# Gated attention plus expert block: the order in which three weight combinations are loaded before the last stage, and two more small products at the start

## The chip, the cores and the metric

The kernel runs on one core of a Trainium2 chip. The metric is device microseconds of one execution, launch to end; lower is better. Before the change three executions took 1855.58, 1856.39 and 1862.57 us (median 1856.39). A fourth, run under the profiler, took 1856.62 us, of which its span (first to last instruction of the program) is 1854.8 us; the other 1.8 us lie around it.

## The reference, cut to what matters

```python
def reference(A_x, A_wqkv, A_wo, B_x, B_w_q, B_k1, B_k2, B_u, B_v, gate_w):
    x = A_x                                        # 1 x 2048 x 1024, f32
    g = _sigmoid((x * gate_w).sum(-1, keepdims=True))
    a = _A_ref(x, A_wqkv, A_wo)                    # 32 heads of 32: softmax(q k^T) v, then @ wo
    b = _B_ref(x, B_w_q, B_k1, B_k2, B_u, B_v)     # 64 experts, one chosen per head, gelu
    return g * a + (1 - g) * b
```

The last operation of `a` is a product of a 2048 x 1024 matrix `o` (the heads' outputs, normalised and gated) with the 1024 x 1024 weight `wo`. `b` ends in a product of a small matrix of expert weights with `v`, added into the same sums.

## The kernel before, in words

All matrix products are done in split precision: an operand is cut into a high part (ScalarE, `split`, L93) and the rest, a low part (VectorE, L94), and a product is high x high + high x low + low x high. So one 128-row product over a depth of 512 is 12 TensorE instructions of 128x512.

**Start.** `wqkv` and `x` arrive in pieces (`load_w0`, `load_x`), are split, and the first projection runs in the loop `mm0` (L213): for each of eight 128-deep slices of `x`, 24 products. The slice `kc=0` goes column block by column block, the others go part by part. While the first pieces travel, TensorE multiplies the identity by itself nine times (L208 and L209; each f32 product of this kind stands as two instructions in the trace). The results are overwritten.

**Middle.** The remaining projections, the expert router, the values, and attention over 32 heads.

**Last stage (from L1154).** The 2048 rows of `o` are done in eight chunks of 256 rows, n = 0 to 7. Chunks 0 and 1 are multiplied plainly by `wo` (`wo_mm`, L1173, into the PSUM banks `pa` and `pa1`; `av_mm`, L1180, adds the expert part). Chunks 2 to 7 go through `unit(n)`: each is a 2x2 block product done with seven block products in place of eight (class `Halves`; `product`, L617). The seven are issued in the order P1, P7, P5, P6, P2, P3, P4 (P3, P4, P2 at the end of the last chunk). Their left factors are blocks of the chunk and sums of blocks, computed and split per chunk (`operand`: A11, S3, S1, A12, S2, S4, A22). Their right factors are blocks of `wo`, which are in SBUF, and four combinations T1 to T4 of blocks of `wo`, made during the values stage, split, and kept in DRAM as `t0h`, `t0l` (T1), `t1h`, `t1l` (T2), `t2h`, `t2l` (T3), `t3h`, `t3l` (T4), high and low part of each. `FACTORS` (L573) pairs them: P7 is S3 with T3, P5 is S1 with T1, P6 is S2 with T2, P4 is A22 with T4.

Each part of a combination is 1 MB (128 rows of 8 KB). `load_t(i, ...)` loads T(i+1) into places that have become free: T1 into the tiles `wo_raw0`, `wo_raw1`, T2 into `wo_raw2`, `wo_raw3` (which held the unsplit `wo`), the high part of T3 into `z0`, its low part into a tile of its own, `t3l`, and T4 into halves of `woh` and `wol`, 512 columns at a time. In the trace the DRAM tensor `t3l` and the tile `t3l` have one name: `t3l<-t2l` loads T3's low part, `wol<-t3l` a piece of T4's.

`load_o(n)` loads chunk n of `o` (tile `V`, eight transfers of 128 KB), `load_rb(n)` its row factors (tile `accd`, four transfers of 256 KB, or small ones for a single slice), `load_at(n)` the expert weights (`at`). `scale_o(n)` multiplies `o` by the factors (L1225). `plain_out(n, pa)` copies the four banks of a plain chunk into the tile `post` (trace: `rb`; L1233 on ScalarE, L1235 on VectorE) and stores it, four stores `out<-rb` of 256 KB. Both plain chunks use the same `post`, so the copies of chunk 1 wait until the stores of chunk 0 have landed. They are called in `unit(2)` after P1 and stand, in the order of both engines, ahead of the operands S2, S4 and A22 of chunk 2.

**Queues.** The order of instructions on each engine is the order of the program, written out by hand. Nearly all loads and stores are issued by SyncE (SP) in one queue; `load_rb(3)` is issued by ScalarE. Every transfer of these two queues takes the next of eight completion counters in turn, and its issue waits until the counter's last user has landed. A waiting issue holds up everything behind it on its queue. Before the change the queue of SP around the change reads: t0h, t0l, t1h, t1l, the eight pieces of chunk 2's `o`, `at`, t2h, t2l, the four stores of chunk 0, the eight pieces of T4, the eight pieces of chunk 3's `o`. The four transfers of `load_rb(3)` take their counters in between: the fourth piece of chunk 2's `o` waits for the first of them, the fifth for the second, the seventh for the third.

The names that the prediction uses: L208/L209 and L213 at the start; `load_t` (L1212), the calls at L1273, L1284 to L1292, `plain_out` (L1230), `unit` (L1310).

Of the kernel before, what the change touches and what calls it, by code (L numbers as in the profile page):

```python
# [10 lines left out]
F32R = mybir.dt.float32r  # L11
# [5 lines left out]
S = 2048  # L17
# [14 lines left out]
def gated_mha_peer_kernel(ctx, tc, xT, wqkv, wv, wo, wq, k12, ug, v, out):  # L32
# [26 lines left out]
    TD = [[dram.tile([128, KC // 2, 512], F32R, name=f"t{i}{part}") for part in "hl"] for i in range(4)]  # L59
# [13 lines left out]
    def dma(dst, src, queue=nc.sync):  # L73
        a, b = (ap.bitcast(F32) if ap.dtype == F32R else ap for ap in (dst, src))
        return queue.dma_start(a, b)
# [76 lines left out]
    def pair(pool, name, m):  # L152
        return [pool.tile([128, m * 512], F32R, name=part + name) for part in ("hi", "lo")]
# [51 lines left out]
    b0 = {(w, n): bank() for w in range(2) for n in range(NQ)}  # L205


    for i in range(9):  # L208
        nc.tensor.matmul(b0[1, NQ - 1][:, :128], ident, ident, start=True, stop=True)  # L209

    def mm0(w, n, kc, i):
# [4 lines left out]
    for kc in range(KC):  # L216
# [17 lines left out]
        for w in range(2):  # L234
            for n, i in order:
                mm0(w, n, kc, i)
            if kc == KC - 1:
                parts = pair(ev0, str(w), NQ)
# [316 lines left out]
    zp = Pool("zp", side="right")  # L555
# [344 lines left out]
    keep = Pool("keep")  # L900

    wo_raw = [keep.tile([128, 2, D], F32, name=f"wo_raw{i}") for i in range(KC // 2)]
# [196 lines left out]
    for h in range(H):  # L1099
        base = h * NT  # L1100
        g, j = divmod(h, 4)
# [52 lines left out]
    fin = Pool("fin")  # L1154
# [9 lines left out]
    def load_at(n):  # L1164
        AT[n] = fin.tile([128, W], F32R, name="at", bufs=3)
        dma(AT[n], ATD[:, n * W:(n + 1) * W])
# [43 lines left out]
    ht = Halves(lambda name: wk.tile([128, 512], F32, name="ssb"), bank)  # L1210

    def load_t(i, *parts):  # L1212

        ht.b[f"T{i + 1}"] = []
        for part, src in zip(parts, TD[i]):
            m = HC // len(part)
            for j, place in enumerate(part):
                dma(place, src[:, m * j:m * j + m, :].rearrange("p k m -> p (k m)"))
            ht.b[f"T{i + 1}"].append([place[:, k * 512:(k + 1) * 512] for place in part for k in range(m)])

    def scale_o(n):

# [20 lines left out]
    def banks4():  # L1243
        return {(i, half): bank() for i in range(W // 128) for half in range(2)}
# [25 lines left out]

    for i in range(2):  # L1273
        load_t(i, *([keep.tile([128, S], F32R, name=f"wo_raw{2 * i + j}")] for j in range(2)))
    ps_odd = Pool("ps_odd", space=PSUM)
    for (i, half), ps in pa.items():
        av_mm(0, i, half, ps)
# [5 lines left out]
        split_o(1, k0, k1)  # L1283
    load_o(2, 0, KC)  # L1284
    load_at(2)
    load_t(2, [zp.tile([128, S], F32R, name="z0")], [fin.tile([128, S], F32R, name="t3l")])
    pa1 = banks4()
    wo_mm(pa1, 1, list(range(KC - 1)), True, False)
    for (i, half), ps in pa1.items():
        av_mm(1, i, half, ps)  # L1290
    plain_out(0, pa)
    load_t(3, *([part[k][:, 512:] for k in range(HC)] for part in (woh, wol)))  # L1292
    load_rb(3, 0, KC, queue=nc.scalar)
    load_o(3, 0, KC)
# [123 lines left out]
```

## Time and profile before

| what | value |
|---|---|
| median of three executions | 1856.39 us |
| the profiled execution | 1856.62 us |
| its span | 1854.8 us |
| TensorE busy in the span | 1843.4 us (99%) |
| VectorE, ScalarE busy | 1365.7 us (74%), 1198.9 us (65%) |
| DMA, mean over the span | 179 GB/s |

How to read it: times are us from the first instruction. PE is TensorE's matmuls, PEld its weight loads, DVE VectorE, ACT ScalarE, SPq and ACTq the issuing of transfers by SyncE and ScalarE. A row of a timeline has the start, the time taken, engine, line, operation, output and inputs, shape and count; in brackets the engine's idle time before it and what ended it. Successive matmuls overlap, so the distance between their starts is their cost, not their stated length. In a table by windows the columns are the window, its length, busy time and count of an engine, the clock that TensorE was granted (1.00 is full), the busy share of the DMA engines and their GB/s.

### The profile page before, as it was taken

What the parts mean: (1) busy time and instruction counts of PE and PEld (TensorE: products, weight loads), DVE (VectorE), ACT (ScalarE), POOL (GpSimd) and SP (SyncE); (2) the same over time, 40 slices, a digit from 0 to 9 for tenths busy, and PEclk for the clock granted to TensorE, in tenths of its full rate; (3) what the DMA queues carried; (4) which work ended last, traced back from release to release, by engine and by line L of the source; (5) the groups of instructions that cost most, each with busy time, mean ns of one, the idle gap of its engine ahead of it and who ended that gap; (6) DMA issues with size and microseconds to landing.
All of it is one profiled execution on the core that took longest, in us unless ns stands there. A gap on an engine that the chain in (4) does not pass through costs nothing.

```text
span 1854.8 us, 26123 instructions
## 1 busy us (share of the span) xinstructions
PE 1843.4 (99%) x10127; PEld 1130.9 (61%) x10127; DVE 1365.7 (74%) x1219; ACT 1198.9 (65%) x1492; POOL 170.1 (9%) x214
## 2 busy tenths in 40 slices
PE   9999999999999999999999999999999999999999
PEld 7877777887888744444444444444444444447787
DVE  4522224978887788888888888888888888895674
ACT  4211111201233399999999999999999999993221
POOL 0000000025401100000000000000000000000000
PEclk9999999999999999999999999999999999999999
DMA  5777784423237687767777777777777777766861
GB/s 215 281 251 255 273 290 135 134 66 104 80 127 247 246 182 160 177 153 176 163 175 176 163 183 170 184 160 183 172 172 169 159 176 177 182 147 196 273 171 57
DMA packets 122853, 332.10 MB, mean 179 GB/s; under 512 B 15988, under 2 KB 57220, under 8 KB 98472
## 3 DMA queue, kind: packets, MB, share of 16 engines
q1 hardware_dynamic: 85048, 180.58, 32.2%
q0 software_dynamic: 17584, 112.08, 28.0%
q10 hardware_dynamic: 20096, 37.76, 6.6%
q8 instruction: 80, 1.31, 0.3%
q14 instruction: 45, 0.37, 0.1%
HBM read 158.65 MB, written 72.10 MB: 124 GB/s over the span
## 4 chain that ended last, share of the span: by engine, by line
PE 85%; issue 6%; DMA 4%; DVE 3%; POOL 1%; ACT 1%; SPq 0%; ACTq 0%; DVEq 0%; POOLq 0%
PE ring L968 28%; PE o L989 25%; PE bk L329 17%; PE pa L617 6%; PE bk L394 3%; PE bk L213 2%; PE bk L274 2%; PE ring L1002 1%; DMA accd<-rd 1%; POOL eq L408 1%; PE pa L1180 1%; DMA t3l<-t2l 1%; DMA rb<-rd 1%; DMA t1l<-xl 1%; DMA smd<-ssb 0%
## 5 line engine op out<-in xcount | busy, mean ns | idle before, releaser
L978 ACT ACTIVATE P<-ring 128x1024 f32<-128x1024 f32 (+2 forms) x1031 | 913.0, 982 | 13.5 <-DMA accd<-P 1.2
L1018 DVE TENSOR_TENSOR acc<-acc,P 128x2048 f32<-128x2048 f32 x319 | 731.0, 2292 | 74.6 <-ACT P L978 49.0
L989 PE MATMUL o<-P,V 128*32 128x512 f32 x3840 | 464.8, 599 | 0.0
L968 PE MATMUL ring<-Q,K 98*128 98x512 f32 x1024 | 272.0, 407 | 0.1
L968 PE MATMUL ring<-z,z 98*128 98x512 f32 x1020 | 270.5, 407 | 0.6 <-ACT accd L978 0.6
L968 PEld LDWEIGHTS ring<-Q,K 98*128 98x128 f32 x1024 | 182.0, 188 | 144.2 <-ACT P L978 72.4
L968 PEld LDWEIGHTS ring<-z,z 98*128 98x128 f32 x1020 | 181.4, 188 | 142.5 <-ACT P L978 72.5
L989 PEld LDWEIGHTS o<-P,V 128*32 128x32 f32 x3840 | 98.8, 109 | 223.3 <-issue 214.4
L93 ACT ACTIVATE hi<-bk 128x512 fp32r<-128x512 f32 x64 | 37.6, 598 | 243.2 <-PE bk L329 227.1
L94 DVE TENSOR_TENSOR lo<-bk,hi 128x512 fp32r<-128x512 f32 x64 | 44.1, 690 | 182.7 <-ACT hi L93 178.5
L329 PE MATMUL bk<-xh,whi 128*128 128x512 f32 x448 | 176.2, 393 | 0.1
L329 PE MATMUL bk<-xh,wlo 128*128 128x512 f32 x448 | 174.4, 389 | 0.0
L329 PE MATMUL bk<-xl,whi 128*128 128x512 f32 x448 | 174.4, 389 | 0.0
L1011 POOL DMA_DIRECT2D accd<-P x95 | 81.5, 858 | 929.4 <-ACT P L978 421.4
L1016 DVE TENSOR_TENSOR acc<-P,P 128x2048 f32<-128x2048 f32 x32 | 73.4, 2293 | 72.9 <-ACT P L978 72.9
L329 PEld LDWEIGHTS bk<-xh,whi 128*128 128x128 f32 x448 | 84.1, 188 | 24.2 <-issue 6.7
L329 PEld LDWEIGHTS bk<-xh,wlo 128*128 128x128 f32 x448 | 84.1, 188 | 17.7
L329 PEld LDWEIGHTS bk<-xl,whi 128*128 128x128 f32 x448 | 84.2, 188 | 16.9
L1021 DVE TENSOR_TENSOR acc<-acc,accd 128x2048 f32<-128x2048 f32 x32 | 73.1, 2285 | 0.0
L978 ACT ACTIVATE accd<-ring 128x1024 f32<-128x1024 f32 (+2 forms) x64 | 62.2, 1032 | 2.5 <-PE ring L968 2.4
L617 PE MATMUL pa<-woh,acc 128*128 128x512 f32 x192 | 62.2, 389 | 0.0
L398 ACT ACTIVATE xu<-bk 128x64 f32<-128x64 f32 x16 | 3.6, 224 | 76.5 <-PE bk L394 71.6
(246 smaller groups left out, 1868.0 us busy)
## 6 DMA issues: line engine op xcount, KB each, us to landing
accd<-P POOLq DMA_DIRECT2D x95, 1024.0 KB, 7.5
wqt<-in_wq SPq DMA_DIRECT2D x32, 1024.0 KB
z<-kdh SPq DMA_DIRECT2D x32, 256.0 KB
z<-qdh SPq DMA_DIRECT2D x32, 256.0 KB
V<-vd SPq DMA_DIRECT2D x32, 256.0 KB
K<-kdh SPq DMA_DIRECT2D x32, 256.0 KB
Q<-qdh SPq DMA_DIRECT2D x32, 256.0 KB
od<-osb SPq DMA_DIRECT2D x32, 256.0 KB
```

The costliest lines, as they stand in the source:

```text
L93: nc.scalar.activation(hi, src, AF.Copy)
L94: (on or nc.vector).tensor_tensor(out=lo, in0=src, in1=hi.bitcast(F32), op=OP.subtract)
L329: nc.tensor.matmul(ps, a[:, kc, :], b[n][:, kc, :], start=first, stop=last)
L394: nc.tensor.matmul(ps, a[t // 4][:, kc, tok], b, start=first, stop=last)
L617: nc.tensor.matmul(ps, self.a[a][i][:, k, :], self.b[b][j][k], start=(not first and k == 0 and i == j == 0), stop=(k == HC - 1 and i == 1))
L968: on_ring(nc.tensor.matmul(ring[:, i, :], K[:98, kt * 128:(kt + 1) * 128], Q[:98, qc * 512:(qc + 1) * 512], start=True, stop=True), i)
L978: on_ring(nc.scalar.activation(P[h, kt][:, q0 * 512:(q0 + m) * 512].rearrange("p (a m) -> p a m", a=m), ring[:, i:i + m, :], AF.Exp, scale ...
L989: nc.tensor.matmul(O[h][32 * qc:32 * qc + 32, :], Vt[g][:, kt, 32 * j:32 * j + 32], p[:, qc * 512:(qc + 1) * 512], start=(kt == 0), stop=( ...
L1011: nc.gpsimd.dma_start(ACCD[h], P[h, kt], accum_op=OP.add)
L1016: nc.vector.tensor_add(ACC[h], P[h, 0], P[h, kt])
L1018: nc.vector.tensor_add(ACC[h], ACC[h], P[h, kt])
L1021: nc.vector.tensor_add(ACC[h], ACC[h], ACCD[h])
```

## The change

Eleven small products in place of nine at L208. `load_t` can load one part of a combination alone. The low part of T3 goes to the head of the group of loads, T1 stays behind it, and T2 moves behind chunk 2's `o`, `at` and the high part of T3. The compiled order on SP becomes: t2l, t0h, t0l, the eight pieces of `o`, `at`, t2h, t1h, t1l, the four stores, T4, chunk 3's `o`. The order on every other engine, and the number and size of the transfers, stay as they are. With the new order the counters fall differently: the fourth piece of `o` waits for t2l, the fifth for the first transfer of `load_rb(3)`, the seventh for the second, t1h for the third, t1l for the fifth piece of `o`; the third transfer of `load_rb(3)` waits for t0h, the fourth for the fourth piece of `o`.

```diff
-    for i in range(9):
+    for i in range(11):
         nc.tensor.matmul(b0[1, NQ - 1][:, :128], ident, ident, start=True, stop=True)
...
     def load_t(i, *parts):

-        ht.b[f"T{i + 1}"] = []
-        for part, src in zip(parts, TD[i]):
+        ops = ht.b.setdefault(f"T{i + 1}", [None, None])
+        for n, (part, src) in enumerate(zip(parts, TD[i])):
+            if part is None:
+                continue
             m = HC // len(part)
             for j, place in enumerate(part):
                 dma(place, src[:, m * j:m * j + m, :].rearrange("p k m -> p (k m)"))
-            ht.b[f"T{i + 1}"].append([place[:, k * 512:(k + 1) * 512] for place in part for k in range(m)])
+            ops[n] = [place[:, k * 512:(k + 1) * 512] for place in part for k in range(m)]
...
-    for i in range(2):
-        load_t(i, *([keep.tile([128, S], F32R, name=f"wo_raw{2 * i + j}")] for j in range(2)))
+    load_t(2, None, [fin.tile([128, S], F32R, name="t3l")])
+    load_t(0, *([keep.tile([128, S], F32R, name=f"wo_raw{j}")] for j in range(2)))
     ps_odd = Pool("ps_odd", space=PSUM)
...
     load_o(2, 0, KC)
     load_at(2)
-    load_t(2, [zp.tile([128, S], F32R, name="z0")], [fin.tile([128, S], F32R, name="t3l")])
+    load_t(2, [zp.tile([128, S], F32R, name="z0")], None)
+    load_t(1, *([keep.tile([128, S], F32R, name=f"wo_raw{2 + j}")] for j in range(2)))
     pa1 = banks4()
```

## The prediction

> **What bounds the kernel now.** I read the page first, then the chain that ended last, then TensorE's own rows around its few pauses.
>
> ```profile
> span 1854.8 us, 26123 instructions
> PE 1843.4 (99%) x10127; PEld 1130.9 (61%) x10127; DVE 1365.7 (74%) x1219; ACT 1198.9 (65%) x1492; POOL 170.1 (9%) x214
> ```
>
> TensorE sets the time; it pauses for 11 us in all. The change can win where it pauses or runs slowly, and its two edits stand at two such places. The chain through the last stage:
>
> ```profile
> 1716.61 9.68 DMA t3l<-t2l
> 1726.29 0.04 issue
> 1726.34 9.84 PE pa L617 x35
> ...
> 1847.70 2.73 PE pa L617 x12
> ```
>
> The transfer of T3's low part, issued at 1716.61, lands at 1726.29 and releases TensorE; from there to the end the chain is TensorE alone. So what P7 of chunk 2 gains, the end gains, unless something else is late by then. TensorE's timeline there:
>
> ```profile
> 1722.54 0.39 PE L617 MATMUL pa<-woh,acc 128*128 128x512 f32 x1
> 1723.92 0.47 PE L617 MATMUL pa<-z,s 128*128 128x512 f32 x1 [0.99 <-ACT osb L1326]
> 1726.34 0.50 PE L617 MATMUL pa<-t3l,s 128*128 128x512 f32 x1 [1.94 <-DMA t3l<-t2l]
> ...
> 1730.54 2.91 PE L617 MATMUL pa<-wo_raw,s 128*128 128x512 f32 x12
> 1733.29 2.88 PE L617 MATMUL pa<-wo_raw,z 128*128 128x512 f32 x12
> ```
>
> P1 ends its issue at 1722.54 + 0.23 = 1722.77 (0.23 us a product: 2.75/12, P5 to P6). P7's first product goes at 1723.92, when t2h has landed (the copy named in the bracket doesn't feed it), the second at 1726.34, and P5 follows at 1730.54. P7 takes 7.77 us in place of 2.72: 5.05 us lost. Of that 3.34 are the two waits against an unbroken stream (1723.92 - 1722.77 and 1726.34 - 1724.15); the other 1.71 is a slower clock:
>
> ```profile
> 1720.14:1723.56 3.42, 2.79 (x13) 1.00 0.99 357
> 1723.56:1726.97 3.41, 1.11 (x4) 1.00 1.01 393
> 1726.97:1730.38 3.41, 3.41 (x10) 0.50 1.05 392
> ```
>
> After a stretch of 3.41 us with TensorE busy 1.11 us (33%) the granted clock is 0.50 for 3.41 us; after one with 82% it stayed at 1.00.
>
> **Part 1: eleven small products.**
>
> ```profile
> 1.40 4.21 PE L209 MATMUL bk<-ident 128*128 128x128 f32 x18 [1.40 <-DVE ident L89]
> 6.68 0.80 PE L213 MATMUL bk<-xh,whi 128*128 128x512 f32 x1 [1.07 <-ACT xh L93]
> 6.66 2.50 DVE L94 TENSOR_TENSOR xl<-xraw,xh 128x512 fp32r<-128x512 f32 x4 [0.23 <-ACT xh L93]
> 8.43 0.63 PE L213 MATMUL bk<-xh,whi 128*128 128x512 f32 x1
> 10.34 0.39 PE L213 MATMUL bk<-xh,wlo 128*128 128x512 f32 x1
> 12.30 2.50 DVE L94 TENSOR_TENSOR xl<-xraw,xh 128x512 fp32r<-128x512 f32 x4 [0.23 <-ACT xh L93]
> 19.43 1.07 PE L213 MATMUL bk<-xh,whi 128*128 128x512 f32 x4
> ...
> 3.24:6.65 3.41, 2.37 (x12) 2.07 (x10) 0.58 (x2) 1.85 (x5) 0.00 (x0) 1.00 1.01 345
> ```
>
> Eighteen recorded products take 4.21 us, 0.234 each; four more end at 1.40 + 22 x 0.234 = 6.55, still before 6.68, so they delay nothing. They can only fill the pause of 1.07 us. The products of the projection run slowly (0.63 us) until about 10 us and quickly (0.39) after it. (The clock column says 1.00 here; the lengths of the rows decide.) The change lies near 10.07. If the clock goes by stretches of 3.41 us, as the rows of the last stage suggest, one ran from 6.65 to there, all busy, and one from 3.24 to 6.65; TensorE was busy 69% of that one and its clock stayed low. With eleven products it would be 97%. If that raises the clock at 6.65, slice 0 is held by VectorE's low parts until 6.66 + 2.50 = 9.16; then 14 products remain, to 12.4. Slice 1 waits for its own low parts, which end at 14.80; 17 of its products (1 + 4 + 12) then remain, 3.9 us, to 18.7, where slice 2 began at 19.43. So the gain is 0.75 us at most, later slices having their data. It is nothing where the stretch lies otherwise against the launch. One execution shows one position only; I take 0.4, ends 0 and 0.75.
>
> The Trainium skill (TensorE: Matmul & The Clock Gate, Part 1: The HAM clock gate) says that this window of about 3.4 us runs freely and doesn't start with the kernel, so that the warm-up differs from run to run; the trace agrees with the length (3.41). By that page the sum is 0 in some executions and -0.75 in others.
>
> **Part 2: the order of the loads.**
>
> ```profile
> 1694.71 0.42 SPq L75 DMA_DIRECT2D wo_raw<-t0h  x1
> 1698.44 0.84 ACTq L75 DMA_DIRECT2D accd<-rd  x2
> 1699.86 0.32 SPq L75 DMA_DIRECT2D V<-od  x1
> 1702.39 0.32 SPq L75 DMA_DIRECT2D V<-od  x1
> 1711.50 0.32 SPq L75 DMA_DIRECT2D V<-od  x1
> 1713.76 0.32 SPq L75 DMA_DIRECT2D V<-od  x1
> ...
> 1716.14 0.38 SPq L75 DMA_DIRECT2D z<-t2h  x1
> 1717.08 3.30 SPq L75 DMA_DIRECT2D out<-rb  x4
> 1723.85 0.32 SPq L75 DMA_DIRECT2D woh<-t3h  x1
> ```
>
> An issue here tells when its counter came free. Piece 2 of `o` goes when t0h has landed (1699.86), piece 3 when t0l has (1702.39): 2.5 us a megabyte. Piece 4 waits for the first transfer of `load_rb(3)`, issued at 1698.44 and landed at 1711.50, 13 us for 256 KB, since it shares the DMA engines with the two megabytes of T2; piece 5 goes 2.3 us later, and t2h only at 1716.14. It lands at 1723.85 (the issue that waited for it), t2l 2.4 later.
>
> In the new order t2l takes t0h's place (lands at 1699.8), t0h 1702.4, and then one megabyte (t0l) shares with `load_rb(3)` in place of two. The two took 9.1 us (1702.39 to 1711.50); half is 4.55, against 2.5 for a megabyte alone. So that first transfer lands 2.5 to 4.5 us sooner, at 1707 to 1709, and with it the pieces of `o`, `at` and t2h: t2h is issued about 3.2 us sooner, near 1712.9, and lands near 1720.6. P7 wants it at 1722.77 and t2l long before: **both waits of P7 go**, and the low clock with them. P5's T1 landed by 1709. If that were all, P6 would start at 1722.77 + 2 x 2.72 = 1728.2 in place of 1733.29: -5.1.
>
> **What is late next** is P6's left factor S2, by the rows of VectorE and ScalarE:
>
> ```profile
> 1727.10 0.69 DVE L1235 COPY rb<-pa 128x512 f32<-128x512 f32 x1 [2.95 <-DMA out<-rb]
> 1728.38 0.69 DVE L1235 COPY rb<-pa 128x512 f32<-128x512 f32 x1 [0.59 <-DMA out<-rb]
> 1728.99 0.68 DVE L599 TENSOR_TENSOR V<-ssb,V 128x512 f32<-128x512 f32 x1
> 1730.37 0.69 DVE L94 TENSOR_TENSOR z<-V,z 128x512 fp32r<-128x512 f32 x1 [0.70 <-ACT z L93]
> ...
> 1729.01 0.60 ACT L1233 ACTIVATE rb<-pa 128x512 f32<-128x512 f32 x1 [0.69 <-DMA out<-rb]
> 1729.71 0.63 ACT L93 ACTIVATE z<-V 128x512 fp32r<-128x512 f32 x1
> ```
>
> S2 stands behind the copies of chunk 1, and these wait for the stores of chunk 0 to land, the last just before 1729.01. S2's low part was ready at 1731.06, hidden behind the slow P7 and P5. P6's third product needs it: wanted at 1728.65, it would wait 2.4 us if the stores landed as before. They start some 3.2 us sooner but with one megabyte more (t1h and t1l in t2l's place) ahead of them, 2.5: a net 0.7; what is left of `load_rb(3)` shares again, and I take 0.5, ends -1 and +2.4 (no wait left). The third product then goes at 1731.06 - 0.5 = 1730.56 in place of 1733.29 + 0.45 = 1733.74: **-3.2**, ends -1.7 and -5.1. T2 lands ahead of the stores, so it isn't the last. Counted at nothing are the loads of T4 and of chunk 3, which keep their places behind the same bytes; P7 of chunk 3 has the cover that these rows show:
>
> ```profile
> 1744.60 2.01 DVE L623 TENSOR_TENSOR rb<-rb,pa 128x512 f32<-128x512 f32 x3
> 1748.71 0.39 PE L617 MATMUL pa<-z,s 128*128 128x512 f32 x1
> ```
>
> Its bank is read by the first of those three, done near 1745.3, so 3.4 us of gain pass even if chunk 3 came no sooner; beyond that TensorE would wait for it.
>
> **Sum.** -3.2 - 0.4 = -3.6 against the profiled execution's 1856.62: 1853.0. The median shown is 0.23 lower, so 1852.8.
>
> **Rivals.**
> - *Everything hidden.* The stores land 2.4 us sooner and P6 doesn't wait: -5.1 - 0.4, 1850.9. For it: the DMA engines were half idle between two bursts and the new order starts the second earlier. Against it: the extra megabyte stands before the stores.
> - *The new wait halves the clock.* P6's pause leaves the stretch from 1726.97 to 1730.38 busy for 1.2 + 0.5 us, about half: between the 33% that dropped the clock and the 82% that didn't. At 0.50 for 3.41 us it costs 1.7: -1.9, 1854.5. By the page named above a whole idle window drops the clock, and this pause is half of one; so it has less than even odds.
> - *The order doesn't matter.* The same bytes are wanted before P6 and the DMA engines are full from 1720 (0.99 to 1.05 above); if T2 and the stores come so late that P6 still starts at 1733.3, only part 1 is left: 1856.0. Against it: S2's own row stands at 1731.06.
> - *Slower: T2 too late.* t1h now waits on SP for the third transfer of `load_rb(3)`, and stores, T4 and chunk 3 wait behind it. It decides once t1l lands after 1733.7 (after 1732.0, should the pause also halve the clock). From an issue near 1714 that is 20 (18) us, where the slowest transfer above took 13; each us beyond costs one, so 2 us late is 1858.4.
>
> **How the numbers follow.** Forecast 0.48, everything hidden 0.21, clock halved 0.16, no effect 0.09, slower 0.06. The range from 1850.4 to 1855.6 holds the first three and leaves the last two and their like out. A measurement of this kernel can tell about 0.5%, 9.3 us, from no change: under 1847.1 or over 1865.7. None of the cases reaches it, the largest being 5.85 us; what I leave for it is for what none of them names, 0.05 faster and 0.03 slower, 0.92 for no change by that bound.
>
> **What would show it.** Right: no wait of TensorE for t2l, P5 starting 2.7 us after P7 at full clock, t2h issued near 1713, a new pause of 1 to 2 us before P6 whose releaser is ScalarE or VectorE, and an unbroken stream behind it. Part 1: lengths of 0.39 from 6.7 us on. Wrong: a wait for T2 at P6, a clock of 0.50 after it, or a wait in chunk 3.

## The result, and the profile after

Ten executions of the changed kernel have a median of 1853.12 us (1851.06 to 1855.39), ten of the kernel before 1857.84 (1855.58 to 1862.57). The ratio is **0.9975, with a 95% interval from 0.9965 to 0.9985**: 4.7 us less, between 2.8 and 6.5. The profiled execution took 1853.26 us; its span is 3.4 us shorter than before.

The head of the page of the changed kernel:

```profile
span 1851.4 us, 26129 instructions
PE 1841.2 (99%) x10131; PEld 1128.1 (61%) x10131; DVE 1365.8 (74%) x1219; ACT 1198.3 (65%) x1492; POOL 170.1 (9%) x214
```

The share of TensorE is 99% as before; a gain of 3 us in 1850 doesn't show in shares. It shows in TensorE's timeline in the last stage (start, time taken, line, operands; in brackets the idle time before and what ended it):

```profile
1722.68 0.39 PE L617 MATMUL pa<-woh,acc 128*128 128x512 f32 x1
1722.90 0.39 PE L617 MATMUL pa<-z,s 128*128 128x512 f32 x1
1723.13 0.39 PE L617 MATMUL pa<-t3l,s 128*128 128x512 f32 x1
...
1725.62 2.88 PE L617 MATMUL pa<-wo_raw,s 128*128 128x512 f32 x12
1729.52 3.30 PE L617 MATMUL pa<-wo_raw,z 128*128 128x512 f32 x12 [1.01 <-ACT z L93]
```

P7 follows P1 without a pause (1722.68, 1722.90, 1723.13: one product each 0.23 us), and P5 comes 2.72 us behind P7 (1722.90 to 1725.62) where it took 6.62 (1723.92 to 1730.54). P6 would have started at 1728.34; it pauses 1.01 us for the high part of its left factor and starts at 1729.52, 1.18 us late. Its third product needs the low part, which VectorE makes in this row:

```profile
1729.50 0.69 DVE L94 TENSOR_TENSOR z<-V,z 128x512 fp32r<-128x512 f32 x1 [0.70 <-ACT z L93]
```

The low part is ready at 1730.19, the third product goes at 1730.24, and P6 takes 3.13 us (to 1732.65) in place of 2.72. So the pause costs 1.6 us in all. From P1's start to the kernel's last product before the final copies and stores it is 126.48 us (1720.18 to 1846.66), against 129.98 (1720.05 to 1850.03): **3.5 us less, and all of the shorter span is here.**

SyncE's issues in the changed kernel (a start tells when the counter came free):

```profile
1708.20 0.32 SPq L75 DMA_DIRECT2D V<-od  x1
...
1711.29 0.38 SPq L75 DMA_DIRECT2D z<-t2h  x1
```

The fifth piece of `o`, which waits for the first transfer of `load_rb(3)`, goes at 1708.20, and t2h at 1711.29 in place of 1716.14: 4.9 us sooner. The chain that ended last goes on from there:

```profile
1715.48 11.94 DMA out<-rb
1727.51 0.69 DVE rb L1237
1728.20 0.61 DVE V L599
1728.83 0.64 ACT z L93
1729.52 3.30 PE pa L617 x12
...
1844.33 2.73 PE pa L617 x12
```

In place of T3's low part, the chain now hangs on a store of chunk 0, which is under way for 11.94 us; then come the copy of a bank of chunk 1, the sum S2, its high part, and P6. Behind it TensorE runs unbroken to the end. The table by windows for this place (window, length, TensorE's busy time and count, granted clock, DMA share, GB/s):

```profile
1724.74:1728.15 3.41, 3.41 (x17) 1.00 0.97 344
1728.15:1731.56 3.41, 2.40 (x10) 1.00 0.91 305
```

The pause leaves TensorE busy 2.40 of 3.41 us, 70%, and the clock stays at 1.00. At the start of the changed kernel:

```profile
1.40 4.08 PE L209 MATMUL bk<-ident 128*128 128x128 f32 x22 [1.40 <-DVE ident L89]
6.68 0.50 PE L213 MATMUL bk<-xh,whi 128*128 128x512 f32 x1 [1.20 <-ACT xh L93]
...
7.97 0.40 PE L213 MATMUL bk<-xh,whi 128*128 128x512 f32 x1
...
18.67 1.07 PE L213 MATMUL bk<-xh,whi 128*128 128x512 f32 x4
...
51.53 0.50 PE L329 MATMUL bk<-xh,whi 128*128 128x512 f32 x1
```

The products take 0.4 us from the third on (before: 0.63 until about 10 us), slice 2 begins at 18.67 in place of 19.43, and the next projection (L329) at 51.53. The same row of the kernel before:

```profile
52.30 0.50 PE L329 MATMUL bk<-xh,whi 128*128 128x512 f32 x1
```

So the start is 0.77 us shorter in these two executions. But P1 of chunk 2 stands at 1720.18 after and 1720.05 before: on the way there the 0.77 us are gone again.

### The profile page after: what moved, and what is told of

Same layout as the page of the kernel before. It is cut to its first block, busy times and chain, and to the rows that moved or that the text cites. A ratio compares the mean times of both kernels' runs of the same rounds, so it can differ in the third digit from the quotient of the medians.

```text
span 1851.4 us, 26129 instructions
## 1 busy us (share of the span) xinstructions
PE 1841.2 (99%) x10131; PEld 1128.1 (61%) x10131; DVE 1365.8 (74%) x1219; ACT 1198.3 (65%) x1492; POOL 170.1 (9%) x214
## 4 chain that ended last, share of the span: by engine, by line
PE 60%; DMA 3%; ACT 1%; DVE 0%; issue 0%; SPq 0%; DVEq 0%; ACTq 0%
PE ring L968 27%; PE o L989 25%; PE pa L617 6%; PE ring L1002 1%; DMA accd<-P 1%; DMA out<-rb 1%; DMA accd<-rd 1%; PE pa L1180 1%; DMA rb<-rd 1%; DMA smd<-ssb 0%; ACT P L978 0%; SPq L75 0%; PE pa L1173 0%; DVE V L1242 0%; DMA V<-od 0%
## 5 line engine op out<-in xcount | busy, mean ns | idle before, releaser
L329 PE MATMUL bk<-xh,whi 128*128 128x512 f32 x448 | 176.2, 393 | 0.1
L329 PE MATMUL bk<-xh,wlo 128*128 128x512 f32 x448 | 174.4, 389 | 0.0
L329 PE MATMUL bk<-xl,whi 128*128 128x512 f32 x448 | 174.4, 389 | 0.0
L329 PEld LDWEIGHTS bk<-xh,whi 128*128 128x128 f32 x448 | 84.1, 188 | 24.1 <-issue 6.7
L329 PEld LDWEIGHTS bk<-xh,wlo 128*128 128x128 f32 x448 | 84.1, 188 | 17.8
L329 PEld LDWEIGHTS bk<-xl,whi 128*128 128x128 f32 x448 | 84.2, 188 | 17.1
```

Of the source, the lines that this page charges most:

```text
L329: nc.tensor.matmul(ps, a[:, kc, :], b[n][:, kc, :], start=first, stop=last)
```

## The experiments

Ratios are to the kernel before, run on the same chip in the same series, with 95% intervals. P1, P7, P5, P6 are the starts of these products of chunk 2. A stretch is one of the 3.41 us for which the clock is constant.

**One edit at a time.** *e1*: the changed kernel with nine small products, so the new order alone.

```diff
-    for i in range(11):
+    for i in range(9):
```

> New order of the loads, nine small products. Theory: the order carries the whole gain at the end: no wait of TensorE for t2l, P7 to P5 2.7 us, a pause of about 1 us before P6, P6 starting 3.5 to 4 us sooner than before; time 3 to 5 us under the kernel before (0.9975). Rival (the small products carry a part that the end sees): 1 us or more slower than with eleven, a gain of 2 to 3 us.

Measured: 0.9976 (0.9967 to 0.9985), median 1852.41 us. *e2*: the kernel before with eleven small products, so the old order.

```diff
-    for i in range(9):
+    for i in range(11):
```

> Old order of the loads, eleven small products. Theory: the start may be 0.77 us shorter, but that is given back by the first head of the attention; P7 waits for t2l as before: within 0.5 us of the kernel before (ratio 0.9998 to 1.0002). Rival: the start's 0.77 us reaches the end, ratio 0.9996; a larger part of the measured gain than that would be a surprise to both.

Measured: 0.9998 (0.9989 to 1.0007), median 1857.06 us. **The order carries the gain**; what eleven products are worth lies inside e2's interval, which reaches 1.7 us to either side. At the start of e1, with nine:

```profile
9.50 0.63 PE L213 MATMUL bk<-xh,whi 128*128 128x512 f32 x1
...
52.52 0.50 PE L329 MATMUL bk<-xh,whi 128*128 128x512 f32 x1
```

The clock is still low at 9.50, as in the kernel before. In e2's last stage (timeline of TensorE):

```profile
1722.53 0.47 PE L617 MATMUL pa<-z,s 128*128 128x512 f32 x1
1725.85 0.50 PE L617 MATMUL pa<-t3l,s 128*128 128x512 f32 x1 [2.85 <-DMA t3l<-t2l]
...
1728.48 2.88 PE L617 MATMUL pa<-wo_raw,s 128*128 128x512 f32 x12
```

TensorE waits 2.85 us for T3's low part, the longest such wait of the old order so far, and yet P7 and P5 run at full speed behind it. The two windows that hold the wait:

```profile
1721.33:1724.74 3.41, 1.67 (x7) 1.00 0.98 365
1724.74:1728.15 3.41, 2.30 (x10) 1.00 1.01 369
```

Busy 49% in the first, 67% in the second: no drop. The same stall thus costs a slow stretch in one execution and none in another, by where the borders of the stretches fall. From P1 to P6 this execution, the fastest of the eleven of e2, took 11.49 us (1719.71 to 1728.48 + 2.72), the profiled one of before 13.24.

**How long does the stall of the old order last?** *e9* and *e10* are the kernel before, unchanged, profiled twice more. Either the 13.24 us are always so, or they vary.

> The kernel before, once more under the profiler. Theory: its stall at P7 of chunk 2 is two waits of together 3 to 3.5 us and, where a stretch of 3.41 us is left with about a third of TensorE's work, a low clock for the next one (1.7 us more). Which stretch that is differs between executions, so P1 to P6 takes either about 13.2 us or about 11.5. Rival (the low clock belongs to the stall itself): 13.2 us each time.

> The kernel before, a third execution, with the same two theories: P1 to P6 either about 13.2 us (low clock) or about 11.5 us, against 13.2 us each time.

Measured: 1859.71 and 1859.48 us. From P1 to P6 14.71 us in e9 (1721.68 to 1736.39) and 15.11 in e10 (1721.05 to 1736.16): longer than either expectation. TensorE in e9:

```profile
1725.48 0.47 PE L617 MATMUL pa<-z,s 128*128 128x512 f32 x1 [0.91 <-DMA z<-t2h]
1728.26 0.79 PE L617 MATMUL pa<-t3l,s 128*128 128x512 f32 x1 [2.31 <-DMA t3l<-t2l]
...
1733.11 3.44 PE L617 MATMUL pa<-wo_raw,s 128*128 128x512 f32 x12
1736.39 2.88 PE L617 MATMUL pa<-wo_raw,z 128*128 128x512 f32 x12
```

and its windows:

```profile
1723.98:1727.39 3.41, 1.05 (x4) 1.00 0.98 378
1727.39:1730.80 3.41, 2.54 (x6) 0.50 1.05 402
1730.80:1734.22 3.42, 3.42 (x9) 0.50 1.05 385
```

Two slow stretches, not one: the wait for t2l reaches into the first of them and leaves it 74% busy (2.54/3.41), and the clock comes back only after the next, which is busy throughout. In the kernel before's first profile the wait ended at 1726.34, ahead of the slow stretch (1726.97), which was then all busy, and one was enough. e10 repeats it:

```profile
1723.76:1727.17 3.41, 0.64 (x2) 1.00 0.96 360
1727.17:1730.58 3.41, 2.54 (x6) 0.50 1.02 387
1730.58:1733.99 3.41, 3.41 (x9) 0.50 0.95 335
```

So four executions of the old order had none (e2), one (before), two (e9) and two (e10) slow stretches. That the stall always takes 13.2 us, the rival of the expectations, falls. e2 ran on another chip than e9 and e10; the medians of the kernel before on the two (1857.46 and 1857.77) agree.

The mean granted clock, which is known of many more executions, agrees. Of 73 executions of the kernel before, 36 have 0.998 (mean time 1858.2 us), 35 have 0.999 (1856.8), one 0.997 and one 1.000; all ten of the changed kernel have 1.000. The three profiles with one, two and two slow stretches have 0.999, 0.998 and 0.998. A low clock behind the last product counts in this mean too, so it doesn't give the number of stretches exactly.

**What holds P6?** *e3*: the changed kernel, with S2 computed ahead of chunk 1's copies.

```diff
+            ht.operand("S2")
             plain_out(1, pa1)
-            for name in ("S2", "S4", "A22"):
+            for name in ("S4", "A22"):
```

> The change, with the operand S2 of chunk 2 ahead of the copies of chunk 1. Theory: the pause before P6 comes from S2 standing behind the copies that wait for the stores; it goes, P6 starts 2.72 us after P5, 1.2 us sooner than with the change alone, and the end with it: about 1.2 us faster (1852 at the median against 1853.1). Rival (P6 waits for T2's own transfers, so the order of the operands is of no use): a wait of about 1 us for t1h or t1l stays, no gain. A third way: the copies, now later, delay S4 and P3, and the gain is given back there.

Measured: 0.9974 (0.9963 to 0.9984), median 1851.8 us. TensorE waits nowhere in the last stage:

```profile
1725.18 2.88 PE L617 MATMUL pa<-wo_raw,s 128*128 128x512 f32 x12
1727.90 2.88 PE L617 MATMUL pa<-wo_raw,z 128*128 128x512 f32 x12
1730.62 0.61 PE L1180 MATMUL pa<-vhl,at 128*128 128x512 f32 x2
```

P5 to P6 and P6 to the next are 2.72 us each. From P1 to the last product it takes 124.93 us, 1.5 less than the changed kernel, which is what its pause cost: the pause came from S2 standing behind the copies, and T2 was there in time. In the median that is too little to tell from the changed kernel (the intervals lie on each other).

**Which part of the order?** *e5*: T2 goes behind `o`, `at` and t2h as in the change, but t2l stays behind t2h.

```diff
-    load_t(2, None, [fin.tile([128, S], F32R, name="t3l")])
     load_t(0, *([keep.tile([128, S], F32R, name=f"wo_raw{j}")] for j in range(2)))
...
-    load_t(2, [zp.tile([128, S], F32R, name="z0")], None)
+    load_t(2, [zp.tile([128, S], F32R, name="z0")], [fin.tile([128, S], F32R, name="t3l")])
     load_t(1, *([keep.tile([128, S], F32R, name=f"wo_raw{2 + j}")] for j in range(2)))
```

> T2 behind chunk 2's o as in the change, but T3's low part stays behind its high part (t0h, t0l, o, at, t2h, t2l, t1h, t1l). Theory: what counts is that T2's two megabytes leave the place ahead of o; where t2l stands is of no matter as long as it lands before 1722.9. o lands near 1709, t2h near 1717, t2l near 1720: no wait at P7, pause of about 1 us before P6 as with the change, time within 0.5 us of it (0.9975). Rival (t2l must be loaded first): a wait of 1 us or more for t2l at P7, gain of 2 us or less.

Measured: 0.9973 (0.9963 to 0.9983), median 1852.84 us. No wait at P7, and almost none at P6:

```profile
1723.06 0.39 PE L617 MATMUL pa<-z,s 128*128 128x512 f32 x1
1723.29 0.39 PE L617 MATMUL pa<-t3l,s 128*128 128x512 f32 x1
...
1728.83 3.29 PE L617 MATMUL pa<-wo_raw,z 128*128 128x512 f32 x12 [0.17 <-ACT z L93]
```

That the pause at P6 is short here is not shown to come from e5's order: with the order of the change it was 1.01 us in the change, 0.85 in e1, 0.25 in e7 and 0.42 in e8.

*e6*: t2l goes to the head as in the change, but T2 stays with T1 ahead of `o`.

```diff
     load_t(2, None, [fin.tile([128, S], F32R, name="t3l")])
-    load_t(0, *([keep.tile([128, S], F32R, name=f"wo_raw{j}")] for j in range(2)))
+    for i in range(2):
+        load_t(i, *([keep.tile([128, S], F32R, name=f"wo_raw{2 * i + j}")] for j in range(2)))
...
     load_t(2, [zp.tile([128, S], F32R, name="z0")], None)
-    load_t(1, *([keep.tile([128, S], F32R, name=f"wo_raw{2 + j}")] for j in range(2)))
```

> T3's low part first as in the change, but T2 stays ahead of chunk 2's o, so five megabytes stand ahead of it. Theory: the eighth piece of o lands near 1720 in place of 1717.6, P1 starts about 2 us late (TensorE waits for A11), t2h lands near 1726 and P7 waits about 1 us more; half or more of the gain is lost: ratio 0.9985 to 0.9995. Rival (loading t2l first is what helped): no wait for o, gain as with the change, 0.9975.

Measured: 0.9991 (0.9982 to 1.0000), median 1855.68 us. With three megabytes more than e5 ahead of `o`, chunk 2 itself is late, and t2h is later still. (The profiled execution, 1859.17 us, is the slowest of the eleven, so its waits may well be longer than usual.)

```profile
1722.83 0.72 PE L617 MATMUL pa<-woh,acc 128*128 128x512 f32 x2 [1.07 <-DVE acc L94]
...
1728.69 0.47 PE L617 MATMUL pa<-z,s 128*128 128x512 f32 x1 [3.27 <-DMA z<-t2h]
```

and e6's windows:

```profile
1725.88:1729.29 3.41, 0.60 (x3) 1.00 1.03 395
1729.29:1732.70 3.41, 3.41 (x10) 0.50 0.89 295
```

The wait for t2h (3.27 us) is longer than expected, and P1 waits for chunk 2, as expected. So **T2 behind `o` is what gains**: with it, T3's low part at the head adds nothing that could be measured (e5 against the change). Without it, the low part at the head may gain something: e6's interval, up to 1.0000, only just reaches no gain. *e11* puts e5 and e3 together.

> T2 behind chunk 2's o with t2l behind t2h (as in the run with that alone), eleven small products, and S2 ahead of the copies of chunk 1. Theory: nothing is left to wait for in the last stage, from P1 of chunk 2 to the last product 125 us (six chunks of 20.85), and the median is at or a little under that of the change, 1851.5 to 1853, a difference that five rounds can hardly show. Rival (a new wait in chunk 2 or 3): 126 us or more.

Measured: 0.9972 (0.9961 to 0.9982), median 1852.54 us, 124.89 us from P1 to the last product, no wait of TensorE in the last stage. With e3's (124.93) it is the shortest way from P1 to the end, and not to be told from the changed kernel by the median.

**The transfers of `load_rb(3)`.** *e4*: the changed kernel, with these four issued by SyncE behind the stores of chunk 0, so that they don't share the DMA engines with T1 and `o`.

```diff
     plain_out(0, pa)
+    load_rb(3, 0, KC)
...
-    load_rb(3, 0, KC, queue=nc.scalar)
```

> The change, with the four transfers of load_rb(3) on SP behind the stores of chunk 0 in place of ScalarE's queue. Theory: chunk 2's o no longer waits for them: its eighth piece lands near 1709 in place of 1712.7, the stores land 2 to 3 us sooner (first copy at 1723 to 1724 in place of 1726.2), S2 is ready before 1728.3 and the pause before P6 goes: 1.2 us faster than the change. Rival (the stores wait for T2's bytes alone): first copy within 0.5 us of 1726.2, pause unchanged. Against both: the factors come late for chunk 3, a new wait at its P1 or P7.

Measured: 0.9982 (0.9973 to 0.9991), median 1854.21 us. VectorE's first copy of chunk 1:

```profile
1720.74 0.69 DVE L1237 COPY rb<-pa 128x512 f32<-128x512 f32 x1 [4.61 <-DMA out<-rb]
```

The store that this copy waits for has landed 0.4 us ahead of P1 (1721.10), where in the changed kernel the same copy starts 6.05 us behind P1 (1726.23 against 1720.18). That is 6.4 us sooner, well over what was expected, and P6 no longer pauses. (The second copy, which waits for a later store, starts at 1723.23, 5.2 us sooner against P1 than its 1727.51 in the changed kernel.) But a list of TensorE's waits shows a new one:

```profile
PE pa L617 <- DVE rb L623: 0.7, 1, 0.7
```

This is P7 of chunk 3, whose bank VectorE still reads: the wait that the expectation named against both theories. VectorE's second product of chunk 3's `o` with its factors starts 17.0 us behind P1 here (1738.11) and 16.0 in e3 (1735.76), and what VectorE does behind it is late with it. From P1 to the last product: 125.86 us, 0.6 less than the changed kernel. The median isn't better (1.2 us less was expected), and its trace reaches P1 0.9 us later; why, no run settles.

**The start.** *e7*: the changed kernel with no small products; *e8*: with sixty.

```diff
-    for i in range(11):
+    for i in range(0):
```

```diff
-    for i in range(11):
+    for i in range(60):
```

> The order of the change, no small products at the start. Theory: the first projection runs at the slow clock until the first full stretch after 6.7 us ends, so 10.1 to 13.5 us; the start loses 0.8 to 2 us against the change, and as much is lost at the first product of the next projection (from 51.5 to 52.3 or later). If the start reaches the end, the median is 1 to 2 us over that of the change; if it is given back on the way (rival), within 0.5 us of it.

> The order of the change, sixty small products at the start in place of eleven: about 120 recorded products, 16 slow ones and the rest at 0.11 us, so that the first product of the projection starts near 16 in place of 6.7 us. TensorE can't catch up, its later slices being a stream at full clock; the next projection starts 7 to 8 us late (59 in place of 51.5). If a delay of the start reaches the end: 7 to 8 us slower than the change (ratio about 1.0015). If the later stages have slack of their own (rival): less than half of it.

Measured: e7 0.9981 (0.9972 to 0.9990), median 1854.09 us; e8 1.0023 (1.0014 to 1.0032), 1861.68. In e7 the next projection starts at 52.55, hardly later than with nine (below), and P1 at 1722.13. In e8:

```profile
1.39 16.24 PE L209 MATMUL bk<-ident 128*128 128x128 f32 x120 [1.39 <-DVE ident L89]
...
61.24 0.50 PE L329 MATMUL bk<-xh,whi 128*128 128x512 f32 x1
```

Its next projection is 9.7 us later than the changed kernel's, P1 (1729.64) 9.5 later, and the median 8.6 higher, a little more than the 7 to 8 expected. **So what the start loses does reach the end**; the stages between make good at most about one of 9.7 us. For a gain of 0.77 us this doesn't show it: TensorE waits 1.8 us in all between the first projection and the last stage of the changed kernel, and a gain could be lost there. Whether the first attention head swallows it stays open.

Set side by side, the starts of all executions say more than any one median. With nine small products the next projection began at 52.30, 52.52, 52.44 and 52.20 us (before, e1, e9, e10), and the products were still at 0.63 us past 9 us in all four. With eleven it began at 51.53, 51.81, 51.59, 52.14, 51.79, 51.78 and 51.35 (the change, e2 to e6, e11), and the products took 0.4 us from 7.5 to 8.0 us on in all seven. The means are 52.37 and 51.71: **0.65 us sooner with eleven.** P1, without e8, starts anywhere from 1719.64 (e1, with nine) to 1722.13 (e7, with none), and nine and eleven aren't sorted in it: the 1670 us between scatter by over two microseconds.

That all of the 0.65 us is the two products' doing isn't shown. The small products themselves show when the clock rises: their records start 0.21 us apart at the low clock and 0.11 apart at the full one. The 22 records take 4.08 us in the changed kernel, but in e4:

```profile
1.39 5.07 PE L209 MATMUL bk<-ident 128*128 128x128 f32 x22 [1.39 <-DVE ident L89]
```

In the changed kernel, e2, e3 and e6 the clock rises at about 4.3, 4.4, 5.1 and 5.5 us. With nine, TensorE is busy until 5.61 as well, so there the stretch that raised the clock would have been as full without the added products. In e5 it rises at about 5.9. Only in e4 and e11 does a stretch end behind the added products, at 7.40 and 6.98, and there it also ends in all four executions with nine (6.65, 7.37, 7.08 and 6.87, one stretch ahead of the rise). e1 with nine and e4 with eleven lie almost alike:

```profile
3.96:7.37 3.41, 2.54 (x10) 1.00 1.04 362
3.99:7.40 3.41, 2.97 (x13) 1.00 1.07 330
```

e1's stretch is 74% busy and the products behind it run slowly; e4's is 87% busy and they run fast. (The clock column says 1.00 for both; as in the prediction, the lengths of the rows decide.) The other three with nine were 69, 72 and 80% busy and stayed slow, e11's was 98% and rose. So in this position the two products do raise the clock one stretch sooner. What nine would do in the other positions no run shows, and so what two products gain on average stays open.

## Why the prediction was right

**Bound, and where the stall goes.** P7's two waits and the slow stretch behind them were the place, and the cause was the one named: t2h and t2l queued behind counters that `load_rb(3)` and T2 held. The first transfer of `load_rb(3)` landed by 1708.20 (forecast 1707 to 1709), t2h was issued at 1711.29, 1.6 us sooner than forecast (near 1712.9), both waits went, and P5 followed P7 after 2.72 us.

**What is late next.** The pause before P6 for S2, behind chunk 1's copies, behind chunk 0's stores, came as forecast: 1.01 us (1 to 2), with ScalarE's high part as its releaser. The stores' gain is right in its size: the first copy starts at 1726.23 in place of 1727.10, 0.87 us sooner where 0.5 was taken. Only the third product was to wait, for the low part; the first waited too, for the high part. The third came at 1730.24, where 1730.56 was forecast. e3 shows the cause by taking it away.

**The rivals.** *Everything hidden* needed S2 2.4 us sooner; P6 had no pause only when S2's place was changed (e3, e11) or `load_rb(3)` was moved (e4), and in e7 little was missing (0.25 us). *The new wait halves the clock*: the stretch around it was 70% busy, not half, and the clock held; what drops it lies lower (49% held in e2, 33% dropped it). *The order doesn't matter* and *T2 too late* fall with e1 and e3: the order alone has all of the gain that can be told, and P6 never waited for T2. *Slower*, which didn't come, leaves part 1's 0.4 us out of its example: by the prediction's own terms 2 us late is 1858.0, not 1858.4.

**Part 1.** The quick products came from the start of the projection, as forecast, in all seven executions with eleven and in none of the four with nine; slice 2 began at 18.67, where 18.7 was forecast. The mechanism, that the two products fill the stretch ahead of the projection, is borne out where the stretch lies as it did in the profile that was read (e4 and e11 against the four with nine). In the changed kernel's own profile the clock rose already at about 4.3 us, not at 6.65, from a stretch that the added products had no part in; so its 0.77 us came by another way than forecast, and that it agrees with the upper end is luck as far as the runs show. Taken at 0.4 us (0 to 0.75), the term is 0.65 at the next projection over all executions. That it depends on the position of the stretch was said; how often it is nothing stays open, because all four executions with nine had their border between 6.65 and 7.37. At the end of the kernel neither e2 nor e1 against the change can resolve it.

**The term that came out too small** is part 2's -3.2. For the profiled execution it fits: -3.5 from P1 to the last product. For the median it is too small, because the stall was read off one execution, which had one slow stretch. From P1 to the last product four executions of the old order (before, e2, e9, e10) took 129.98, 128.22, 131.44 and 131.84 us, on average 130.4; four with the new order (the change, e1, e7, e8) took 126.48, 126.31, 125.71 and 125.92, on average 126.1. That is -4.3. Measured at the median was -4.7 (2.8 to 6.5), an interval that holds the forecast of -3.6 too.

The forecast time, 1852.8, is nearer to the measured 1853.12 than the gain is, and that is luck: it was set against the median of three executions, 1856.39, where ten give 1857.84. The base was 1.45 us too low and the gain 1.1 too small. e9 and e10 show that another profile of the same kernel stands 3 us higher, 1.5 to 1.9 us of it in this stall.

**Counted at nothing and paid for.** Chunk 3's P7 was said to have 3.4 us of cover even if chunk 3 came no sooner. Nothing waits there in the change, nor in e3 and e11, where P7 comes 5 us sooner against P1 of chunk 2 than before and chunk 3 sooner with it. In e4, where VectorE came to chunk 3's `o` 1 us later against P1 than in e3, the cover was used up and P7 waited 0.7 us.

## What to carry to other kernels

Where transfers of two queues take turns on a few counters, ask of each load which counter it waits for: a small load that shares the DMA engines with a bulk one can hold back everything behind it, and it is the bulk that isn't wanted yet that should move back. A stall on TensorE costs the wait and then a number of slow stretches that differs from execution to execution, so it is sized from several profiles of the same kernel, not from one. A gain of half a microsecond is better looked for where it arises, in the starts of several traces, than in the median at the end; and where the clock has its own stretches, their position in each trace has to be read too, or it is counted as the change's.

## What the runs showed of the hardware

**When the clock drops and when it comes back.** At 1.00, a stretch of 3.41 us that was 18% (e6), 19% (e10), 31% (e9) or 33% busy (before) was followed by 0.50; one of 49% and 67% (e2), 70% (the change) or 82% (before) wasn't. At 0.50, a stretch that was 74% busy (e9, e10) was followed by another slow one; one that was all busy ended it (before, e6, e9, e10). At the start 69 to 80% (before, e1, e9, e10) left the products slow, 87% (e4) and 98% (e11) made them fast. So a stall can cost none, one or two slow stretches. The Trainium skill (TensorE: Matmul & The Clock Gate, Part 1: The HAM clock gate) has the array go cold after at least one idle window of about 3.4 us, and says that the window runs freely; the traces agree with the length (3.41 us) and with the free run (a stretch ends at 6.65 us after the first instruction in before, at 7.37 in e1, at 7.08 in e9), but a window that is a third busy already drops the clock here.

**A small transfer beside a bulk one.** 256 KB on ScalarE's queue took 13 us from issue to landing beside T1 and T2 (before: 1698.44 to 1711.50). With that group of transfers moved behind the stores (e4), the first copy that waits for the stores of chunk 0 starts 6.4 us sooner against P1 than in the changed kernel.
